# A spectral filter in front of a squared-ReLU FFN: the FFT rebuilt on conjugate pairs, the FFN in 512-token groups over batch borders, one written-out instruction order

## The chip, the cores and the metric

The kernel runs on one core of one Trainium2 chip. The metric is the device time of one execution in microseconds; lower is better. The core has five engines that each work off an instruction list of their own in order: TensorE (PE in the rows; its weight loads are listed apart as PEld), VectorE (DVE), ScalarE (ACT), GpSimd (POOL) and SyncE (SP, which here only issues DMA transfers). They wait for one another through semaphores.

## What is computed

Eight batches of 3008 tokens of 256 channels. Along the tokens of each batch a real FFT is taken, multiplied by a complex filter (one row for each of 1505 frequencies), and transformed back. All 24064 tokens then go through an FFN with a squared ReLU.

```python
def _attn_ref(x, filt_r, filt_i):                 # x: (8, 3008, 256)
    X = np.fft.rfft(x, axis=1)
    F = (filt_r + 1j * filt_i)[None, :, :]        # (1, 1505, 256)
    y = np.fft.irfft(X * F, n=x.shape[1], axis=1)
    return y.astype(np.float32)

def _moe_ref(x, w_in, w_out):                     # (24064, 256), (256, 2048), (2048, 256)
    h = np.maximum(x @ w_in, 0.0)
    return (h * h @ w_out).astype(np.float32)
```

Inputs and output are float32; matmul operands are float16 and sums float32 in both kernels.

## The kernel before

**The FFT as matmuls.** 3008 = 64 x 47. A token is n = 64 n2 + n1, a frequency k = 47 k1 + k2. Every step is a matmul against a constant table:

- *A* (L249, into psA): over n2. x is loaded in four pieces of a batch as x32 (48 rows x 16 x 256 float32, 768 KB, SP, L157), cast to x16 by VectorE (L163, 47x4096), and multiplied by sSA (47x48), 512 columns at a time, 32 matmuls for each batch. ACT copies psA to u (L251), and SP writes u to a DRAM scratch dU (L253, pieces of 384 KB).
- dU is read back with n1 on partitions as ut (L257, two transfers of 768 KB for each batch, in runs of 512 bytes).
- *B* (L275 and L277, into psB): for each of 47 values of k2 two matmuls with 64 output rows and 256 columns, the same table sSB, into the lower and the upper half of psB; 94 for each batch. VectorE multiplies psB by the filter sF into prod (L284, two k2 in one instruction of 128x512). The real Nyquist frequency takes a path of its own (L281, L289, L301).
- *P* (L298, into psP): the inverse over k1, 47 matmuls for each batch; VectorE copies psP to zeta (L302), SP writes it to DRAM as dZ (L304, four transfers of 768 KB).
- dZ is read back as ztw (L308, two transfers of 192 KB for each of eight pieces), and *Y* (L322, into psY) does the inverse over k2: 128 matmuls of 47 columns for each batch. ACT (L326) and VectorE (L329) copy psY to yt, which is the FFN's input with channels on partitions.

**The FFN.** For each batch alone, in groups of 256 tokens (TOKG), 12 to a batch, of which the last has 192. Eight steps g1 with 4 matmuls of 256 columns into psH (L182, two buffers), ACT's relu from psH to h2 (L187), VectorE's square of h2 in place after every second step (L190, 128x1024); then g2, 32 matmuls into psO (L203, one buffer), ACT's copy to ost (L210) and the write to out on ACT's queue (L211).

**The order.** The FFN of batch b-1 is a generator of such steps. While the code of batch b's FFT is written out, `drain(prev, 1)` takes one FFN step after each FFT matmul group, and what is left of the FFN at the end of a batch is written out as one piece; A of batch b needs the x loaded during batch b-1. The tile scheduler may then put instructions of an engine in another order, as its readiness rules have it. Tables and filters are loaded ahead of everything: sSA, sSB, sSBp, sNY, sSAp and then x on SP, the filters (four transfers, since real and imaginary part each stand twice) and the FFN's weights on POOL's queue.

Of the kernel before, what the change touches and what calls it, by code (L numbers as in the profile page):

```python
# [11 lines left out]
AOP = mybir.AluOpType  # L13
# [63 lines left out]
def kernel(
# [27 lines left out]
    p_xin = ctx.enter_context(tc.tile_pool(name="p_xin", bufs=2))  # L105
    p_x16 = ctx.enter_context(tc.tile_pool(name="p_x16", bufs=2))
    p_u = ctx.enter_context(tc.tile_pool(name="p_u", bufs=2))
    p_ut = ctx.enter_context(tc.tile_pool(name="p_ut", bufs=1))
    p_xsb = ctx.enter_context(tc.tile_pool(name="p_xsb", bufs=2))
    p_prod = ctx.enter_context(tc.tile_pool(name="p_prod", bufs=2))  # L110
    p_nyq = ctx.enter_context(tc.tile_pool(name="p_nyq", bufs=1))
    p_zeta = ctx.enter_context(tc.tile_pool(name="p_zeta", bufs=2))
    p_ztw = ctx.enter_context(tc.tile_pool(name="p_ztw", bufs=2))
    p_y = ctx.enter_context(tc.tile_pool(name="p_y", bufs=2))
    p_h2 = ctx.enter_context(tc.tile_pool(name="p_h2", bufs=2))
    p_out = ctx.enter_context(tc.tile_pool(name="p_out", bufs=2))

    sSA = const.tile([47, 48], F16, name="sSA")
    nc.sync.dma_start(out=sSA, in_=dSA.ap())
    sSB = const.tile([128, 47, 66], F16, name="sSB")  # L120
    nc.sync.dma_start(out=sSB, in_=dSB.ap().rearrange("p (a b) -> p a b", b=66))
    sSBp = const.tile([128, 47, 128], F16, name="sSBp")
    nc.sync.dma_start(out=sSBp, in_=dSBp.ap().rearrange("p (a b) -> p a b", b=128))
    sNY = const.tile([1, 128], F16, name="sNY")
    nc.sync.dma_start(out=sNY, in_=dNY.ap())
    sSAp = const.tile([96, 47], F16, name="sSAp")
    nc.sync.dma_start(out=sSAp, in_=dSAp.ap())

    fr3 = filt_r[0:1504, :].rearrange("(k1 k2) d -> k1 k2 d", k2=47)
    fi3 = filt_i[0:1504, :].rearrange("(k1 k2) d -> k1 k2 d", k2=47)  # L130
    sF = const.tile([128, 47, D], F16, name="sF")
    nc.gpsimd.dma_start(out=sF[0:32], in_=fr3)
    nc.gpsimd.dma_start(out=sF[32:64], in_=fi3)
    nc.gpsimd.dma_start(out=sF[64:96], in_=fi3)
    nc.gpsimd.dma_start(out=sF[96:128], in_=fr3)
    sFnyq = const.tile([1, D], F16, name="sFnyq")
    nc.gpsimd.dma_start(out=sFnyq, in_=filt_r[1504:1505, :])

    sWin = const.tile([128, 2, DFF], F16, name="sWin")
    nc.gpsimd.dma_start(out=sWin, in_=moe_w_in.rearrange("(t r) j -> r t j", r=128))  # L140
    sWout = const.tile([128, NJT, 256], F16, name="sWout")
    nc.gpsimd.dma_start(out=sWout, in_=moe_w_out.rearrange("(jt r) c -> r jt c", r=128))

# [222 lines left out]
```

## Time and profile before

| | us |
|---|---|
| runs, median of 3 | 1231.53 |
| runs, lowest to highest | 1229.78 to 1232.30 |
| the profiled execution, first to last instruction (its span) | 1228.8 |
| PE busy in it | 1027.7 |
| ACT busy | 636.9 |
| VectorE busy | 601.2 |

The profile is one execution, and its page gives its span as its time; that is 2.7 us under the median of the runs. "Busy" counts the time in which at least one instruction of the engine is under way. Matmuls are pipelined: the time listed for a group of back-to-back matmuls runs from the first one's start to the last one's modelled end, which lies after the end of its columns. A row's bracket tells how long the engine had been idle before it, and which instruction or transfer ended that.

### The profile page before, as it was taken

The page shows a single profiled execution, that of the slowest core. Times are in us where ns is not written, and L with a number is a line of the kernel's source. Part 1 is how long each engine was busy: PE and PEld are TensorE (multiplying, and loading weights), DVE is VectorE, ACT ScalarE, POOL GpSimd, SP SyncE. Part 2 cuts the span into 40 slices and gives each one's busy share as a digit, 9 for nine tenths or more (in the row PEclk, how much of TensorE's full clock was granted, in tenths as well). Part 3 has the DMA queues.
Part 4 walks back from the last instruction along what each step waited for, and adds up shares of the span by engine and source line. Part 5 has one row for each costly group of instructions (what it writes and reads, how often), then busy time and mean ns, then how long its engine had stood idle before and what let it go on. Part 6 is the DMA issues. An engine that isn't in the chain of part 4 may idle for free.

```text
span 1228.8 us, 20376 instructions
## 1 busy us (share of the span) xinstructions
PE 1027.7 (84%) x8568; PEld 703.8 (57%) x8568; DVE 601.2 (49%) x880; ACT 636.9 (52%) x1193; POOL 4.7 (0%) x11
## 2 busy tenths in 40 slices
PE   0328549999699979997999959997999989997887
PEld 0002115777477757765666637665666757676776
DVE  0216625464257733764359533774358524753332
ACT  0224116665465646455754745555664665455564
POOL 1000000000000000000000000000000000000000
PEclk9999999999799979998999959998899979998999
DMA  9974685135502576127362683146542460242011
GB/s 215 174 159 96 160 147 126 59 93 129 131 27 78 160 151 124 70 94 177 77 117 95 156 172 65 64 131 145 115 77 104 130 144 27 78 129 76 28 34 33
DMA packets 113621, 134.08 MB, mean 109 GB/s; under 512 B 5886, under 2 KB 105726, under 8 KB 110206
## 3 DMA queue, kind: packets, MB, share of 16 engines
q1 hardware_dynamic: 85242, 102.96, 37.1%
q10 hardware_dynamic: 25728, 24.65, 6.3%
q0 software_dynamic: 2560, 5.18, 2.6%
q8 instruction: 67, 1.10, 0.4%
q14 instruction: 24, 0.20, 0.1%
HBM read 75.55 MB, written 62.39 MB: 112 GB/s over the span
## 4 chain that ended last, share of the span: by engine, by line
PE 68%; DMA 12%; ACT 10%; DVE 7%; issue 2%; SPq 1%; ACTq 0%; DVEq 0%
PE psO L203 26%; PE psH L182 23%; ACT h L187 6%; PE psA L249 5%; PE psB L275 5%; DMA x<-in_x_dram 5%; DMA ztw<-dZ 4%; PE psP L298 4%; DVE h L190 3%; PE psY L322 3%; DMA dU<-u 2%; DMA ut<-dU 2%; DVE x L163 1%; ACT u L251 1%; ACT ost L210 1%
## 5 line engine op out<-in xcount | busy, mean ns | idle before, releaser
L187 ACT ACTIVATE h<-psH 128x512 f16<-128x512 f32 (+1 forms) x768 | 433.7, 588 | 154.5 <-PE psH L182 139.6
L182 PE MATMUL psH<-yt,sWin 128*128 128x256 f16 (+1 forms) x3072 | 455.2, 277 | 21.0 <-ACT h L187 15.1
L203 PE MATMUL psO<-sWout,h 128*128 128x256 f16 (+1 forms) x3072 | 418.7, 273 | 8.5 <-DVE h L190 2.4
L190 DVE TENSOR_TENSOR h<-h 128x1024 f16<-128x1024 f16 (+1 forms) x384 | 257.7, 675 | 288.3 <-ACT h L187 287.9
L182 PEld LDWEIGHTS <-sWin 128*128 128x128 f16 x3072 | 290.7, 100 | 111.9 <-issue 72.4
L203 PEld LDWEIGHTS <-h 128*128 128x128 f16 (+1 forms) x3072 | 284.7, 98 | 83.6 <-DVE h L190 35.7
L251 ACT CAST u<-psA 48x512 f16<-48x512 f32 x256 | 141.4, 574 | 124.9 <-PE psA L249 87.6
L284 DVE TENSOR_TENSOR prod<-psB,sF 128x512 f16<-128x512 f32 x192 | 130.1, 678 | 100.2 <-PE psB L277 58.6
L249 PE MATMUL psA<-x,sSA 47*48 47x512 f16 x256 | 110.4, 472 | 65.2 <-DVE x L163 40.4
L210 ACT COPY ost<-psO 128x512 f32<-128x512 f32 x88 | 51.5, 585 | 198.1 <-PE psO L203 198.1
L302 DVE CAST zeta<-psP 128x512 f16<-128x512 f32 x192 | 129.1, 673 | 23.5 <-PE psP L298 22.8
L163 DVE CAST x<-x 47x4096 f16<-47x4096 f32 x32 | 73.0, 2282 | 88.5 <-DMA x<-in_x_dram 48.2
L322 PE MATMUL psY<-sSAp,ztw 96*128 96x47 f16 x1024 | 54.5, 199 | 73.4 <-DMA ztw<-dZ 48.5
L275 PE MATMUL psB<-ut,sSB 128*64 128x256 f16 x376 | 85.5, 306 | 25.1 <-DMA ut<-dU 22.6
L322 PEld LDWEIGHTS <-ztw 96*128 96x128 f16 x1024 | 44.6, 106 | 103.2 <-issue 57.2
L329 DVE CAST yt<-psY 128x376 f16<-128x376 f32 x64 | 35.0, 547 | 119.1 <-PE psY L322 119.1
L249 PEld LDWEIGHTS <-sSA 47*48 47x48 f16 x256 | 22.9, 105 | 114.9 <-issue 105.4
L277 PE MATMUL psB<-ut,sSB 128*64 128x256 f16 x376 | 86.4, 308 | 0.0
L298 PE MATMUL psP<-prod,sSBp 128*128 128x256 f16 x376 | 81.0, 294 | 3.6 <-DVE zeta L302 3.2
L326 ACT CAST yt<-psY 128x376 f16<-128x376 f32 x64 | 30.2, 471 | 94.6 <-PE psY L322 93.3
L275 PEld LDWEIGHTS <-sSB 128*64 128x64 f16 x376 | 29.3, 112 | 71.1 <-issue 70.9
L298 PEld LDWEIGHTS <-sSBp 128*128 128x128 f16 x376 | 33.5, 99 | 25.1 <-issue 16.6
(21 smaller groups left out, 51.3 us busy)
## 6 DMA issues: line engine op xcount, KB each, us to landing
dZ<-zeta SPq DMA_DIRECT2D x32, 768.0 KB, 3.5
ztw<-dZ SPq DMA_DIRECT2D x128, 192.0 KB, 3.4
out_dram<-ost ACTq DMA_DIRECT2D x88, 256.0 KB, 2.2
x<-in_x_dram SPq DMA_DIRECT2D x28, 768.0 KB, 9.2
dU<-u SPq DMA_DIRECT2D x32, 384.0 KB, 4.6
ut<-dU SPq DMA_DIRECT2D x16, 768.0 KB, 9.3
x<-in_x_dram SPq DMA_DIRECT2D x4, 512.0 KB, 8.1
sF<-in_filt_r_dram POOLq DMA_DIRECT2D x2, 752.0 KB, 16.9
```

The source lines that it names most:

```text
L182: nc.tensor.matmul(ps[:, i, 0:tg], sWin[:, dt, jt * 128:(jt + 1) * 128], yt[:, dt, t0:t0 + tg], start=(dt == 0), stop=(dt == 1))
L187: nc.scalar.activation(out=h2[:, jt0:jt0 + 2, 0:tg], in_=ps[:, :, 0:tg], func=AF.Relu)
L190: nc.vector.tensor_mul(out=h2[:, jt0 - 2:jt0 + 2, 0:tg], in0=h2[:, jt0 - 2:jt0 + 2, 0:tg], in1=h2[:, jt0 - 2:jt0 + 2, 0:tg])
L203: nc.tensor.matmul(ps[0:tw, h, :], h2[:, jt, h * 128:h * 128 + tw], sWout[:, jt, :], start=(jt == 0), stop=(jt == NJT - 1))
L249: nc.tensor.matmul(ps, sSA, xt[:, n1a:n1a + 2, :], start=True, stop=True)
L251: nc.scalar.copy(out=u[:, 2 * i:2 * i + 2, :], in_=ps.rearrange("p (a d) -> p a d", d=D))
L275: nc.tensor.matmul(psb[0:64, i, :], sSB[:, k2, 0:64], ut[:, c2, :], start=True, stop=True)
L277: nc.tensor.matmul(psb[64:128, i, :], sSB[:, k2, 0:64], ut[:, c2, :], start=True, stop=True, tile_position=(0, 64))
L284: nc.vector.tensor_mul(out=prod[:, 0:n, :], in0=psb[:, 0:n, :], in1=sF[:, 2 * p:2 * p + n, :])
L298: nc.tensor.matmul(psp[:, i, :], sSBp[:, k2, :], prod[:, i, :], start=True, stop=(k2 != 0))
L302: nc.vector.tensor_copy(out=zeta[:, 2 * pp:2 * pp + n, :], in_=psp[:, 0:n, :])
L322: nc.tensor.matmul(psy[:, j, :], ztc[:, j, dt * 128:(dt + 1) * 128], sSAp, start=True, stop=True)
```

## The change

**FFT.** A token is now n = 32 p + m, m = 0..31 and p = 0..93, that is n1 = 32 h + m with h = p mod 2. x32 has 96 rows x 8 x 256 (768 KB again, 8 KB to a row); x16 is 94x2048; A is 16 matmuls of 94x96 for each batch, and its psA (96x512) is copied by ACT for even units and by VectorE for odd ones. k2 and 47-k2 are taken together as a pair c (24 pairs): their frequencies f fill 64 rows, real and imaginary part 128. B is 24 matmuls of 128x128 by 256 columns. VectorE multiplies psB by the filter in both of its orders (sF now 128 x 2 x 24 x 256, its second order built on the core by four copies of 64x3072), one instruction of 128x1024 for two pairs, psB read twice. P is 48 matmuls of 128x128 by 256 columns, two that add up for each pair; ACT copies psP to ze. dZ shrinks from 128x48x256 to 3072x256 elements. Y is 64 matmuls of 94 columns for each batch. Nyquist sits in row 32 of pair 0, and its path of its own is gone. In bytes loaded at the start: x of batch 0 3.1 MB, tables sSB and sSP 2.4 MB (now on ACT's queue), filters 1.5 MB and FFN weights 2.1 MB in float16 (POOL's queue).

**FFN.** 47 groups of 512 tokens (TG) over all batches; a group over a batch border is split into two column pieces. g1 has 4 matmuls of 512 columns into psH (128x1024, two buffers), one relu of 1024 elements; the square is one instruction for each step; g2 is 8 matmuls of 256 columns into psO (two buffers), for the group before. Output goes out on SP's queue.

**Order.** `manual_schedule` keeps every engine's list as the code writes it. The FFT of batch 0 runs alone. Then 384 slots run, 8 to a group; a slot is ffn_g1, an FFT unit (place 0), ffn_g2 of the group before, an FFT unit (place 1), the output copy if any, the square. The FFT of a batch is laid over 39 slots by `fft_plan`: A in slots 0 to 7, dU's read-back in 8, B in 13 to 24 and P in 14 to 25, dZ's read-back in 27, Y in 31 to 38; it starts at the group in which the batch before begins to be used up.

```diff
-N1 = 64
-N2 = 47
-NK1 = 33
-TOKG = 256
+N1, N2, NC, NM = 64, 47, 24, 32
+TG = 512
+SLOTS = 8
...
+    ctx.enter_context(tc.manual_schedule())
...
+    def psF(name):
+        return pps.tile([128, 512], F32, tag="psF", name=name, bufs=2)
...
+    load_x(0, 0)
+    load_x(0, 1)
+    sSB = const.tile([128, NC, 128], F16, name="sSB")
+    nc.scalar.dma_start(out=sSB, in_=dSB.ap().rearrange("p (a b) -> p a b", b=128))
...
+    def unit_a(b, a):
+        c, i = divmod(a, 4)
+        if i == 0:
+            cast_x(b, c)
+            us[(b, c)] = p_u.tile([96, 8, D], F16, tag="u", name=f"u_{b}_{c}")
+        ps = psF(f"psA_{b}_{a}")
+        nc.tensor.matmul(ps[0:96, :], sSA, x16s[(b, c)][:, 2 * i:2 * i + 2, :],
+                         start=True, stop=True)
...
+        if a % 2 == 0:
+            nc.scalar.copy(out=o, in_=pv)
+        else:
+            nc.vector.tensor_copy(out=o, in_=pv)
+        if i == 3:
+            nc.sync.dma_start(
+                out=dU[b].rearrange("(m q) d -> q m d", q=96)[:, 8 * c:8 * c + 8, :],
+                in_=us.pop((b, c)))
...
+    def read_u(b):
+        ut = p_ut.tile([128, NC, D], F16, tag="ut", name=f"ut_{b}")
+        v = dU[b].rearrange("(p s) d -> p s d", s=NC)
+        for s0, s1 in ((0, 8), (8, 24)):
+            nc.sync.dma_start(out=ut[:, s0:s1, :], in_=v[:, s0:s1, :])
+        uts[b] = ut
...
+        nc.vector.tensor_mul(
+            out=prod,
+            in0=ps.rearrange("p (a d) -> p a d", d=D).unsqueeze(1).to_broadcast([128, 2, 2, D]),
+            in1=sF[:, :, 2 * p:2 * p + 2, :])
...
+        for i in range(2):
+            for v in range(2):
+                nc.tensor.matmul(ps[:, i * D:(i + 1) * D], sSP[:, 2 * p + i, v, :],
+                                 prod[:, v, i, :], start=(v == 0), stop=(v == 1))
...
+        for i in range(2):
+            jt = 2 * s + i
+            for o, b, r, n in segs:
+                for dt in range(2):
+                    nc.tensor.matmul(ps[:, i, o:o + n],
+                                     sWin[:, dt, jt * 128:(jt + 1) * 128],
+                                     yts[b][:, dt, r:r + n],
+                                     start=(dt == 0), stop=(dt == 1))
+        nc.scalar.activation(out=h2[:, 2 * s:2 * s + 2, :], in_=ps, func=AF.Relu)
...
+    def ffn_g2(g, s):
+        t, half = divmod(s, 2)
+        if s % 4 == 0:
+            pso[g] = pps.tile([128, 2, 256], F32, tag="psO", name=f"psO_{g}_{s}", bufs=2)
+        for jt in range(8 * half, 8 * half + 8):
+            nc.tensor.matmul(pso[g][:, t % 2, :], h2s[g][:, jt, t * 128:(t + 1) * 128],
+                             sWout[:, jt, :], start=(jt == 0), stop=(jt == NJT - 1))
...
+        for a in range(16):
+            if a % 4 == 0 and a // 4 + 2 < 4:
+                put(a // 2, 0, load_x, b, a // 4 + 2)
+            put(a // 2, a % 2, unit_a, b, a)
+        put(8, 1, read_u, b)
+        for p in range(12):
+            put(13 + p, 0, unit_b, b, p)
+            put(14 + p, 1, unit_p, b, p)
+        for c in range(4):
+            put(27, 1, read_z, b, c)
...
+        for n in range(16):
+            put(31 + n // 2, n % 2, unit_y, b, n)
...
+    for s in range((NG + 1) * SLOTS):
+        g, k = divmod(s, SLOTS)
+        if g < NG:
+            ffn_g1(g, k)
+        run(work, s, 0)
+        if g > 0:
+            ffn_g2(g - 1, k)
+        run(work, s, 1)
+        if g > 0:
+            ffn_out(g - 1, k)
+        if g < NG:
+            ffn_sq(g, k)
```

**VectorE around a cast of x.** Before, in the FFN of batch 0 (x16_3_0 is the cast of batch 3's first piece, h2 the squares, prod the filter products):

```order
L267 MEMSET zeta_1_3_1780 128x128
L190 TENSOR_TENSOR h2_0_5_1368<-h2_0_5_1368 128x1024
L163 CAST x16_3_0_2391<-x32_3_0_2389 47x4096
L190 TENSOR_TENSOR h2_0_5_1368<-h2_0_5_1368 128x1024
L190 TENSOR_TENSOR h2_0_6_1513<-h2_0_6_1513 128x1024 x3
L284 TENSOR_TENSOR prod_1_15_1650<-psB_1_15_1645,sF_109 128x512
L190 TENSOR_TENSOR h2_0_6_1513<-h2_0_6_1513 128x1024
```

After, in slots 0 to 3 of batch 2's A (u is the copy of an odd psA, h2 the square that closes a slot, x16_2_1 the cast of the second piece):

```order
L203 CAST u_2_0_1371<-psA_2_1_1384 96x512 [waits DMAHW3_49,PE_49]
L297 TENSOR_TENSOR h2_5_1356<-h2_5_1356 128x1024 [waits Activation_49]
L203 CAST u_2_0_1371<-psA_2_3_1409 96x512 [waits PE_49]
L297 TENSOR_TENSOR h2_5_1356<-h2_5_1356 128x1024 [waits Activation_49]
L186 CAST x16_2_1_1426<-x32_2_1_1079 94x2048 [waits DMAHW6_49]
L203 CAST u_2_1_1428<-psA_2_5_1440 96x512 [waits DMAHW4_49,PE_49]
L297 TENSOR_TENSOR h2_5_1356<-h2_5_1356 128x1024 [waits Activation_49]
L203 CAST u_2_1_1428<-psA_2_7_1465 96x512 [waits PE_49]
```

The cast stood far ahead of the A that uses it, among squares and products; it now stands behind the odd copy and the square of the slot before and directly ahead of its A.

**PE around that A.** Before, in a mix of FFN of batch 1 and A of batch 3 (psH and sWin belong to the FFN):

```order
L182 MATMUL psH_1_8_4_3497<-yt_1_735,sWin_116 128x256
L182 LDWEIGHTS sWin_116
L182 MATMUL psH_1_8_4_3497<-yt_1_735,sWin_116 128x256
L249 LDWEIGHTS sSA_99
L249 MATMUL psA_3_1_1_4169<-x16_3_1_2474,sSA_99 48x512
L182 LDWEIGHTS sWin_116
L182 MATMUL psH_1_8_5_3508<-yt_1_735,sWin_116 128x256
L182 LDWEIGHTS sWin_116
```

After, in slot 2 of batch 2's A, at a group over the border of batches 0 and 1 (448 and 64 columns; h2_4 is the group before):

```order
L289 LDWEIGHTS sWin_135
L289 MATMUL psH_5_2_1414<-yt_1_1118,sWin_135 128x64
L196 LDWEIGHTS sSA_111
L196 MATMUL psA_2_4_1429<-x16_2_1_1426,sSA_111 96x512
L304 LDWEIGHTS h2_4_1143
L304 MATMUL psO_4_0_1375<-sWout_137,h2_4_1143 128x256
L304 LDWEIGHTS h2_4_1143
```

An A matmul stood wherever the scheduler found it ready; it now stands between g1 and g2 of a fixed slot.

**SP between A and B.** Before (u_2_3 is the last piece of batch 2's A, ut its read-back):

```order
L308 DMA ztw_1_7_2218<-dZ1_129 48x8x256 [waits DMAHW4_49,DMAHW3_49,PE_49]
L308 DMA ztw_1_7_2218<-dZ1_129 48x8x256 [waits DMAHW0_49]
L253 DMA dU2_122<-u_2_3_2701 48x4096 [waits DMAHW1_49,Activation_49]
L257 DMA ut_2_2822<-dU2_122 64x24x256 [waits DMAHW1_49]
L257 DMA ut_2_2822<-dU2_122 64x24x256
L304 DMA dZ2_130<-zeta_2_0_2868 128x3072 [waits DVE_49]
```

After, at the same place of batch 2:

```order
L205 DMA dU2_97<-u_2_2_1485 96x8x256 [waits DMAHW7_49,DVE_49,Activation_49]
L205 DMA dU2_97<-u_2_3_1540 96x8x256 [waits DMAHW0_49,DVE_49,Activation_49]
L313 DMA out_0_dram<-ost_4_7_1581 128x2x256 [waits DMAHW1_49,Activation_49]
L213 DMA ut_2_1601<-dU2_97 128x2048 [waits DMAHW3_49,DMAHW5_49,DMAHW2_49,DMAHW7_49,DMAHW0_49,PE_49]
L213 DMA ut_2_1601<-dU2_97 128x4096
L313 DMA out_0_dram<-ost_5_3_1649 128x2x256 [waits DMAHW4_49,Activation_49]
```

Output writes have moved onto SP, ahead of and behind the read-back, which waits for the four writes of dU.

## Rows read from the trace of the kernel before

**Rows 1.** The page: busy time of PE and PEld, and the chain by engine.
```profile
PE 1027.7 (84%) x8568; PEld 703.8 (57%) x8568; DVE 601.2 (49%) x880; ACT 636.9 (52%) x1193; POOL 4.7 (0%) x11
...
PE 68%; DMA 12%; ACT 10%; DVE 7%; issue 2%; SPq 1%; ACTq 0%; DVEq 0%
```

**Rows 2.** Timeline, first FFT: start, length, engine, line, instruction [idle before].
```profile
34.42 2.29 DVE L163 CAST x<-x 47x4096 f16<-47x4096 f32 x1 [34.42 <-DMA x<-in_x_dram]
...
94.02 0.39 PE L275 MATMUL psB<-ut,sSB 128*64 128x256 f16 x1 [20.64 <-DMA ut<-dU]
```

**Rows 3.** All psH matmuls: min/median/max ns, first and last start.
```profile
L182 PE MATMUL psH<-yt,sWin x3072: 242/272/422, 196.0 to 1220.8; 128*128 128x256 f16 x176, 128*128 128x192 f16 x16
```

**Rows 4.** Windows: length; PE, PEld, DVE, ACT, POOL busy; granted clock, DMA share, GB/s.
```profile
196.00:330.00 134.00, 121.78 (x1067) 89.70 (x1065) 66.61 (x102) 75.30 (x141) 0.00 (x0) 0.95 0.46 112
1125.00:1229.00 104.00, 89.43 (x752) 70.97 (x750) 31.98 (x47) 58.46 (x106) 0.00 (x0) 0.99 0.09 31
```

**Rows 5.** Timeline of the end, where only the FFN runs.
```profile
1195.37 0.27 PE L203 MATMUL psO<-sWout,h 128*128 128x256 f16 x1
...
1197.49 2.36 PE L203 MATMUL psO<-sWout,h 128*128 128x256 f16 x20
...
1199.89 0.58 ACT L210 COPY ost<-psO 128x512 f32<-128x512 f32 x1 [1.97 <-PE psO L203]
...
1206.04 2.36 PE L203 MATMUL psO<-sWout,h 128*128 128x256 f16 x20
...
1222.18 2.47 PE L203 MATMUL psO<-sWout,h 128*128 128x256 f16 x20 [0.41 <-DVE h L190]
```

**Rows 6.** Timeline, PE alone, where A and Y of two batches meet.
```profile
438.66 0.61 PE L249 MATMUL psA<-x,sSA 47*48 47x512 f16 x2
...
442.02 0.36 PE L322 MATMUL psY<-sSAp,ztw 96*128 96x47 f16 x8 [0.24 <-ACT yt L326]
```

**Rows 7.** Instructions grouped by shape: busy us, mean ns of one, idle before.
```profile
L187 ACT ACTIVATE h<-psH 128x512 f16<-128x512 f32 x704 | 404.0, 597 | 150.4 <-PE psH L182 136.5 <-DVE prod L284 1.0 <-DVE h L190 0.7
...
L182 PEld LDWEIGHTS <-sWin 128*128 128x128 f16 x3072 | 290.7, 100 | 111.9 <-issue 72.4
...
L190 DVE TENSOR_TENSOR h<-h 128x1024 f16<-128x1024 f16 x352 | 240.1, 686 | 259.7 <-ACT h L187 259.5
L251 ACT CAST u<-psA 48x512 f16<-48x512 f32 x256 | 141.4, 574 | 124.9 <-PE psA L249 87.6 <-DMA dU<-u 30.1 <-DMA ztw<-dZ 4.0
L284 DVE TENSOR_TENSOR prod<-psB,sF 128x512 f16<-128x512 f32 x184 | 126.7, 689 | 91.3 <-PE psB L277 58.0 <-PE psP L298 29.0
...
L163 DVE CAST x<-x 47x4096 f16<-47x4096 f32 x32 | 73.0, 2282 | 88.5 <-DMA x<-in_x_dram 48.2 <-PE psA L249 40.3
...
L187 ACT ACTIVATE h<-psH 128x384 f16<-128x384 f32 x64 | 29.7, 491 | 4.1 <-PE psH L182 3.0
```

**Rows 8.** Timeline, VectorE alone: squares back to back.
```profile
296.06 1.74 DVE L190 TENSOR_TENSOR h<-h 128x1024 f16<-128x1024 f16 x3
```

**Rows 9.** DMA issues: count, KB each, median us from issue to landing.
```profile
dZ<-zeta SPq DMA_DIRECT2D x32, 768.0 KB, 3.5
ztw<-dZ SPq DMA_DIRECT2D x128, 192.0 KB, 3.4
...
x<-in_x_dram SPq DMA_DIRECT2D x28, 768.0 KB, 9.2
dU<-u SPq DMA_DIRECT2D x32, 384.0 KB, 4.6
ut<-dU SPq DMA_DIRECT2D x16, 768.0 KB, 9.3
```

**Rows 10.** Windows, columns as in rows 4: the first 20 us.
```profile
0.00:20.00 20.00, 0.00 (x0) 0.11 (x1) 0.00 (x0) 1.28 (x1) 4.71 (x11) 1.00 0.92 223
```

**Rows 11.** Windows, columns as in rows 4: two stretches with gaps on PE.
```profile
300.00:310.00 10.00, 7.51 (x85) 5.61 (x83) 2.22 (x4) 5.01 (x11) 0.00 (x0) 1.00 0.77 140
440.00:450.00 10.00, 4.23 (x66) 2.96 (x65) 3.42 (x5) 2.95 (x6) 0.00 (x0) 0.62 0.54 140
```

More of the change, by code (lines that the diff above doesn't have):

```diff
@@ new lines, in _build_consts @@
+    m = np.arange(NM)
+    SA = np.zeros((N2, 2, 2, 2, NC))
+    for c in range(NC):
+        for h in range(2):
+            SA[:, h, h, 0, c] = np.cos(2 * np.pi * n2 * c / N2)
+            SA[:, h, h, 1, c] = np.sin(2 * np.pi * n2 * c / N2)
+    freq = np.full((NC, 64), -1)
+    for c in range(NC):
+        for j in range(32):
+            freq[c, j] = 47 * j + c
+            if c:
+                freq[c, 32 + j] = 47 * j + 47 - c
+    freq[0, 32] = N // 2
+    SB = np.zeros((NM, 2, 2, NC, 2, 64))
@@ L76 @@
+    SY = np.zeros((2, 2, NC, N2, 2))
+    for c in range(NC):
+        th = 2 * np.pi * c * n2 / N2
+        for i in range(2):
+            SY[i, 0, c, :, i] = np.cos(th)
+            SY[i, 1, c, :, i] = -np.sin(th)
+    f16 = lambda a, p: np.ascontiguousarray(a.reshape(p, -1).astype(np.float16))
+    return f16(SA, 94), f16(SB, 128), f16(SP, 128), f16(SY, 96)
 @with_exitstack
@@ L124 @@
[L124 to L134, printed above, removed]
@@ new lines, with ffn_g1 @@
+    h2s, pso = {}, {}
+    def ffn_g1(g, s):
+        if s == 0:
+            h2s[g] = p_h2.tile([128, NJT, TG], F16, tag="h2", name=f"h2_{g}")
+        h2 = h2s[g]
+        ps = pps.tile([128, 2, 512], F32, tag="psH", name=f"psH_{g}_{s}", bufs=2)
+        segs = []
+        t = g * TG
+        while t < (g + 1) * TG:
+            b, r = divmod(t, S)
+            n = min((g + 1) * TG - t, S - r)
+            segs.append((t - g * TG, b, r, n))
+            t += n
+        for i in range(2):
+            jt = 2 * s + i
[6 more added lines that the diff above has]
+        nc.scalar.activation(out=h2[:, 2 * s:2 * s + 2, :], in_=ps, func=AF.Relu)
@@ new lines, in run @@
+    def run(plan, r, place):
+        for f, a in plan.get((r, place), ()):
+            f(*a)
+    plan0 = fft_plan(0)
+    for r in range(41):
+        if r == 12:
+            for c0, c1 in ((0, 12), (12, 24)):
+                nc.vector.tensor_copy(out=sF[0:64, 1, c0:c1, :], in_=sF[64:128, 0, c0:c1, :])
+                nc.vector.tensor_copy(out=sF[64:128, 1, c0:c1, :], in_=sF[0:64, 0, c0:c1, :])
+        run(plan0, r, 0)
+        run(plan0, r, 1)
+    work = {}
+    for b in range(1, B):
+        first = 0 if b == 1 else ((b - 1) * S // TG) * SLOTS
+        for (r, place), w in fft_plan(b).items():
+            work[(first + r, place)] = w
```

379 lines of the change are left out of this document (133 added, 246 removed).

## The prediction

> **What bounds the kernel now.** I read the page's busy line and chain first. PE is busy 1027.7 of 1228.8 us and the chain of waits gives it 68%, DMA 12% and ACT 10% [rows 1]; what limits it depends on the stage, so I cut the span into stages. Three are to be seen. **First**, nothing of the FFN runs before 196.0 us: x reaches VectorE at 34.4 us, the first B matmul starts at 94.0 us after 20.6 us of waiting for the read-back of dU [rows 2], and the first psH matmul comes at 196.0 us [rows 3]. **Second**, the last 104 us are FFN alone [rows 4], at 8.55 us for 256 tokens: the same run of 20 psO matmuls starts at 1197.49 and 1206.04 us [rows 5]. Those 20 take 2.36 us; the modelled tail of the last is 0.16 us (one alone shows 0.27), so one 256-column matmul costs 0.110 us, and the 64 matmuls of 256 tokens are worth 7.0 us. The missing 1.5 us is PE waiting while ACT clears psH. **Third**, one batch of FFN with the next batch's FFT inside takes some 130 us, PE busy 122 of 134 at a mean granted clock of 0.95 [rows 4]. So PE bounds it in the middle, with too many matmuls there and some holes; round trips through DRAM bound the beginning.
>
> **The change part by part.** From here "slot" is one turn of the new loop: ffn_g1, an FFT unit, ffn_g2, an FFT unit. All sums are for the profiled execution (span 1228.8 us), and 2.7 us are added at the end, the distance from it to the median of the runs (1231.5).
>
> *FFN matmuls.* A slot has 4 matmuls of 512 columns and 8 of 256. Two psA matmuls of 512 columns take 0.61 us [rows 6], less the tail 0.45, so 0.22 each, the same per column as psO. So g1 costs 4 x 0.218 = 0.87 us, g2 8 x 0.109 = 0.87 us, and 376 slots of both (g2 runs one group behind, so that the last 8 slots have only g2 and the first 8 only g1) 376 x 1.747 = **657 us**. Groups of 512 over batch borders remove the 192-token remainders; seven groups are split at a border, into pieces of 64 columns at least. For these and for reaching the high clock I put **6 us** (0 to 12).
>
> *FFT matmuls.* Per batch now 16 psA of 512 columns (32 before), 24 psB of 256 (94 half-wide ones before), 48 psP, 64 psY of 94. With 0.218, 0.109, 0.109, and for psY 0.045 (eight of 47 columns take 0.36 us with the tail [rows 6], 0.025 each; twice the columns cannot be under 0.039), this is 3.5 + 2.6 + 5.2 + 2.9 = 14.2 us, for the seven batches that run inside the FFN **100 us**.
>
> *A rule against this.* Twelve new weight loads stand in each slot, and a load lasts 100 ns in its rows [rows 7]. The 20 psO matmuls each have a load of their own and still come every 0.110 us [rows 5], so loads lie beside matmuls and I cost them at nothing. The Trainium skill ("TensorE: Matmul & The Clock Gate", the section on row/col tiling) says that a load overlaps matmuls in flight only when the row group differs; by that each load here would add its full time. The trace disagrees; what the sum would be by it stands with the rivals.
>
> *What ACT and VectorE must do in a slot.* Relu of 512 elements takes 597 ns and of 384 491 ns [rows 7], 0.83 ns for one more, so 1024 take 1.02 us. ACT has this, one copy (574 ns for 512 elements [rows 7]) and every fourth slot an ost copy: 1.75 us at most. VectorE has the square (686 ns) and in B/P a product of 1024 elements: 689 ns for 512 [rows 7], so at most 1.38 us; together 2.07 us at most. PE's slot is 1.75 us without FFT, 2.18 with A, 2.4 with B and P, 2.15 with Y. In B/P a product starts 0.22 us after its matmuls (ost starts 0.22 us after the last psO has streamed [rows 5]) and ends 1.4 us later, 0.6 us ahead of the matmul that takes its buffer again. There PE stays the bound. ACT is under it everywhere, so that the 1.5 us holes of the tail close: the relu of a slot has the g2 of the same slot beside it.
>
> *The A stretch is another matter.* VectorE's list there is odd copy, square, odd copy, square, cast, and so on, with one cast in two slots. The odd copy needs the slot's last matmul, the square stands behind it, the cast behind that, and the first psA matmul of the next slot needs the cast. PE has only g1 to fill the time, and behind the waiting psA are queued g2 and the whole slot. From the end of the odd matmul: 0.22 to the copy, 0.53 (a PSUM source of 512 elements, the product's 689 ns, less 0.16, since three squares of 686 ns back to back take 1.74 us, 0.53 apart [rows 8]), 0.53 for the square, and a cast of 94x2048, half of the 2282 ns of 47x4096 [rows 7], say 1.2 us: 2.48 us, of which g1 covers 0.87. PE waits 1.6 us. The first cast of a batch has no odd copy ahead of it: the square ends some 1.0 us into the slot, the cast at 2.2, PE wants it at 0.87: 1.3 us. That is 1.3 + 3 x 1.6 = 6.1 us for each of six batches and 4.8 for batch 1: **41 us**. Bounds: 0 if the order on VectorE let the cast through, 55 with no overlap between its instructions.
>
> *DRAM round trips inside the FFN.* After A there are five slots without FFT work, 8.7 us, and g1, 0.9: 9.6 us for the last odd copy (0.9), the dU write (4.6 median) and the first third of ut. ut lands 9.3 us after issue (median of 768 KB pieces), dU 4.6 [rows 9]; the new first piece is 512 KB in rows of 4 KB instead of 512 B, estimate 5 us from there. 10.9 + issue against 9.6: 1.5 us of waiting for each batch, **10 us** (0 to 40). After P the same five slots stand against 0.8 + 3.5 + 3.4 [rows 9]: covered. x pieces (9.2 us) have some 10 us: covered, barely. While SP waits for dU, an out write is queued behind it; three ost buffers of four slots each cover that.
>
> *The first FFT.* x now comes first on SP, the tables on ACT's queue, half as much filter on POOL's. The first 20 us of before move 223 GB/s [rows 10]. 3.1 MB of x alone would be there at 14 us, with all that loads beside it (9.1 MB) at 41; the third and fourth pieces wait for casts, I take 30. A 3, dU and ut 11, B/P 13 turns of 2.0 us (matmuls at half clock 0.43, 0.22, product 1.38) 26, dZ and zt 8, Y 9, and 5 for transfers that share queues: first psH matmul at **92 us** (73 to 115) instead of 196. The filter copies lie in the dU/ut round trip. **End**: last psO to the end of the span now takes 4 us (1222.18 + 2.47 - 0.16 against 1228.8 [rows 5]): **4 us**.
>
> **Sum:** 92 + 657 + 6 + 100 + 41 + 10 + 4 = 910, with the 2.7 us 913 us.
>
> **The rivals.**
> *The casts cost nothing* (the term of 41 falls away, because VectorE is ahead of PE in the A stretch). For it: VectorE's work in two A slots is 3.9 us against PE's 4.4. Against: order, not load, makes the wait. 872 us.
> *Round trips are exposed.* If all of ut must land (9.3 us) before B and zt needs 9 us (its median is 3.4), PE waits 5.5 and 4.5 us for each batch: 70 instead of 10 us, 973 us. For it: PE waited 20.6 us for ut in the first FFT [rows 2].
> *The clock falls in the A stretch*, where I forecast PE busy for about 70% of the time. Granted clock was 1.00 in a stretch with PE busy 7.51 of 10 us, 0.62 (both levels, 1.2 and 2.4 GHz, mixed) with 4.23 [rows 11]; 70% is nearer to the first. At 1.2 GHz eight slots take 17.5 us more, the waits 3.9 less: 82 us for six batches and 8 for batch 1, 1003 us. The Trainium skill (the same page, on oscillation of the clock) describes matmul loops in which a wait in every turn brings the clock down; by it this rival would be the likelier one, but the middle of this trace keeps 1.00 in most stretches with short holes.
> *Slower than before: the weight loads are not hidden.* Place: all 376 slots, with 12 loads of 100 ns, 451 us, and 152 loads for each of seven FFTs, 106 us: 1470 us. It decides from 57% exposed on (319 of 557 us). Against it stand the 0.110 us above.
>
> **How the numbers follow.** Forecast 57%, casts free 15%, round trips 14%, clock 9%, loads 2%, anything else 3%. The range goes from 860 (casts free and the first FFT at 80) to 1000 (round trips and the first FFT at 115), which leaves out the clock, the loads and some of the rest, 15% or so. All but the loads and part of the rest are faster by hundreds of us, far from the 0.2% that a measurement can tell: faster 0.97, within 0.2% 0.01, slower 0.02.
>
> **What would show it.** First psH matmul near 92 us; B/P and plain slots of 2.4 and 1.75 us with PE without holes; in the A stretch PE waiting for the cast, 1.6 us, 21 times, plus the batches' first ones; PE waits for ut under 2 us; granted clock 1.00 from the first FFN slots on. Wrong would be: a first psH after 115 us, PE waits for psH's relu, waits of over 4 us for ut or zt, or a clock under 0.95 in the A stretches.

## The result and the profile after

The changed kernel takes 898.4 us (median, 897.6 to 898.6) against 1231.3 us: 0.729 of the time before, interval 0.727 to 0.731. The forecast was 913 us, within 860 to 1000. The profiled execution spans 896.8 us, 1.6 us under the median of the runs.

The page of the changed kernel, the lines that answer to [rows 1]:

```profile
PE 792.4 (88%) x5952; PEld 552.6 (62%) x5952; DVE 479.1 (53%) x636; ACT 543.6 (61%) x695; POOL 7.9 (1%) x17
...
PE 84%; DVE 6%; DMA 5%; issue 2%; ACT 2%; SPq 0%; DVEq 0%; ACTq 0%
```

PE now makes 84% of the chain, VectorE 6%. All psH matmuls in one row (the answer to [rows 3]), then the stretch in which FFN and FFT run together (windows, columns as in [rows 4]):

```profile
L289 PE MATMUL psH<-yt,sWin x1728: 191/379/634, 91.5 to 884.8; 128*128 128x512 f16 x143, 128*128 128x64 f16 x8, 128*128 128x320 f16 x8, 128*128 128x128 f16 x7
```
```profile
92.00:885.00 793.00, 750.90 (x5729) 527.90 (x5728) 445.29 (x600) 524.21 (x662) 0.00 (x0) 1.00 0.37 112
```

The FFN begins at 91.5 us instead of 196.0, and from there PE is busy 751 of 793 us with the granted clock at 1.00 (2.4 GHz). The column hides that the first 4 us still ran at half of that; the last section comes back to it. Who waited for whom in that part of the span (from 92 us on): engine, for whom, us in total, times, longest:

```profile
ACT h L293 <- PE psH L289: 203.7, 341, 2.4
...
PE psA L196 <- DVE x L186: 41.9, 27, 1.7
...
PE psH L289 <- DVE yt L268: 0.2, 1, 0.2
```

PE's matmuls wait there for one thing, the cast of x: three times in batch 1 and four times in each later batch. The A stretch of batch 2, first on PE, then on VectorE:

```profile
187.70 1.04 PE L289 MATMUL psH<-yt,sWin 128*128 128x448 f16 x8
190.37 0.42 PE L196 MATMUL psA<-x,sSA 94*96 94x512 f16 x1 [1.64 <-DVE x L186]
...
203.62 1.03 PE L289 MATMUL psH<-yt,sWin 128*128 128x512 f16 x4
...
205.36 1.03 PE L289 MATMUL psH<-yt,sWin 128*128 128x512 f16 x4
```
```profile
187.90 0.69 DVE L203 CAST u<-psA 96x512 f16<-96x512 f32 x1 [0.91 <-PE psA L196]
188.50 0.68 DVE L297 TENSOR_TENSOR h<-h 128x1024 f16<-128x1024 f16 x1
189.10 1.22 DVE L186 CAST x<-x 94x2048 f16<-94x2048 f32 x1
191.92 0.69 DVE L203 CAST u<-psA 96x512 f16<-96x512 f32 x1 [1.60 <-PE psA L196]
```

Odd copy, square and cast run one behind the other, with 0.91 and 1.60 us of idle time on VectorE around them: it is not short of time, it is late. The cast ends at 190.32, psA starts at 190.37. Six slots on, without FFT, one slot is 205.36 - 203.62 = 1.74 us and PE has no hole. Instructions by shape and DMA issues, the answers to [rows 7] and [rows 9]:

```profile
L293 ACT ACTIVATE h<-psH 128x1024 f16<-128x1024 f32 x376 | 385.1, 1024 | 206.0 <-PE psH L289 203.7 <-DVE h L297 2.2
...
L186 DVE CAST x<-x 94x2048 f16<-94x2048 f32 x32 | 38.9, 1217 | 23.2 <-DMA x<-in_x_dram 23.2
```
```profile
x<-in_x_dram SPq DMA_DIRECT2D x28, 768.0 KB, 9.1
dU<-u SPq DMA_DIRECT2D x32, 384.0 KB, 3.4
...
ut<-dU SPq DMA_DIRECT2D x8, 1024.0 KB, 6.1
ut<-dU SPq DMA_DIRECT2D x8, 512.0 KB, 3.7
```

### The profile page after: what moved, and what is told of

It is laid out like the page before. It is cut to its first block, busy times and chain, and to the rows that moved or that the text cites. A ratio compares the mean times of both kernels' runs of the same rounds, so it can differ in the third digit from the quotient of the medians.

```text
span 896.8 us, 14010 instructions
## 1 busy us (share of the span) xinstructions
PE 792.4 (88%) x5952; PEld 552.6 (62%) x5952; DVE 479.1 (53%) x636; ACT 543.6 (61%) x695; POOL 7.9 (1%) x17
## 4 chain that ended last, share of the span: by engine, by line
PE 84%; DVE 6%; DMA 5%; issue 2%; ACT 2%; SPq 0%; DVEq 0%; ACTq 0%
PE psO L304 36%; PE psH L289 34%; PE psP L236 5%; DVE x L186 4%; DMA x<-in_x_dram 4%; PE psA L196 3%; PE psB L219 3%; PE psY L259 3%; DVE h L297 2%; ACT ze L238 1%; ACT h L293 1%; DMA dU<-u 1%; DVE u L203 1%; DMA ut<-dU 0%; DMA zt<-dZ 0%
## 5 line engine op out<-in xcount | busy, mean ns | idle before, releaser
L293 ACT ACTIVATE h<-psH 128x1024 f16<-128x1024 f32 x376 | 385.1, 1024 | 206.0 <-PE psH L289 203.7
L304 PE MATMUL psO<-sWout,h 128*128 128x256 f16 x3008 | 388.6, 272 | 0.0
L289 PE MATMUL psH<-yt,sWin 128*128 128x512 f16 (+7 forms) x1728 | 388.1, 352 | 0.2 <-DVE yt L268 0.2
L297 DVE TENSOR_TENSOR h<-h 128x1024 f16<-128x1024 f16 x376 | 258.0, 686 | 188.8 <-ACT h L293 188.8
L304 PEld LDWEIGHTS <-h 128*128 128x128 f16 x3008 | 291.5, 98 | 83.1 <-issue 6.9
L289 PEld LDWEIGHTS <-sWin 128*128 128x128 f16 x1728 | 159.8, 98 | 100.6 <-issue 2.0
L222 DVE TENSOR_TENSOR prod<-psB,sF 128x1024 f16<-128x1024 f32 x96 | 117.4, 1224 | 57.6 <-PE psB L219 56.6
L196 PE MATMUL psA<-x,sSA 94*96 94x512 f16 x128 | 51.4, 421 | 73.9 <-DVE x L186 72.4
L238 ACT CAST ze<-psP 128x512 f16<-128x512 f32 x96 | 56.2, 585 | 68.0 <-PE psP L236 68.0
L201 ACT CAST u<-psA 96x512 f16<-96x512 f32 x64 | 36.9, 577 | 57.8 <-PE psA L196 56.8
L236 PE MATMUL psP<-prod,sSP 128*128 128x256 f16 x384 | 63.0, 290 | 1.6 <-DVE prod L222 0.9
```

What stands on the lines that cost most here:

```text
L196: nc.tensor.matmul(ps[0:96, :], sSA, x16s[(b, c)][:, 2 * i:2 * i + 2, :], start=True, stop=True)
L222: nc.vector.tensor_mul(out=prod, in0=ps.rearrange("p (a d) -> p a d", d=D).unsqueeze(1).to_broadcast([128, 2, 2, D]), in1=sF[:, :, 2 * p:2 ...
L236: nc.tensor.matmul(ps[:, i * D:(i + 1) * D], sSP[:, 2 * p + i, v, :], prod[:, v, i, :], start=(v == 0), stop=(v == 1))
L238: nc.scalar.copy(out=zes[(b, c)][:, 2 * i6:2 * i6 + 2, :], in_=ps.rearrange("p (a d) -> p a d", d=D))
L289: nc.tensor.matmul(ps[:, i, o:o + n], sWin[:, dt, jt * 128:(jt + 1) * 128], yts[b][:, dt, r:r + n], start=(dt == 0), stop=(dt == 1))
L293: nc.scalar.activation(out=h2[:, 2 * s:2 * s + 2, :], in_=ps, func=AF.Relu)
```

## The experiments

Theory: after the change PE's matmuls set the time from 91.5 us on, and the only thing added to them is the wait for the cast, which comes from its place in VectorE's order. Each run has its rival in what was expected of it.

**The cast, one slot earlier** (each cast of a piece c goes to slot 2c-1, ahead of that slot's copy and square).

```diff
         if i == 0:
-            cast_x(b, c)
             us[(b, c)] = p_u.tile([96, 8, D], F16, tag="u", name=f"u_{b}_{c}")
...
+        for c in range(4):
+            put(max(2 * c - 1, first), 0, cast_x, b, c)
...
```

> The cast of each x piece stands one slot earlier on VectorE, ahead of that slot's odd copy and square; nothing else is moved. Theory (PE waits for the cast because of its place in VectorE's order: 41.9 us of psA waits behind casts in the FFN part of the changed kernel): those waits go, and unless another wait takes their place the median falls from 898 to about 857 us. What may be late next are the x pieces 2 and 3 of a batch: their load is issued behind casts 0 and 1, lands 9.1 us later, and the shorter slots leave about 8.7 us; at 2 us for each of seven batches that gives 868 us. Rival (VectorE's amount of work in the A stretch, not its order, holds PE): the waits stay with the copies, 890 us or more.

Measured: 855.1 us (854.6 to 858.2). PE's waits from 95 us on:

```profile
PE psA L195 <- DVE x L186: 1.3, 1, 1.3
PE psA L195 <- DVE u L202: 0.4, 2, 0.2
PE psA L195 <- ACT u L200: 0.3, 1, 0.3
```

41.9 us have become 1.3, and the time fell by 43.3. VectorE does the same work as before, so its amount was not the cause. Nothing was given back. Four casts waited for their x piece, 0.8 us at most, and PE's one wait for a cast is these 1.3 us.

**Casts and x loads far earlier.**

```diff
...
-            cast_x(b, c)
...
+        for c, r in enumerate((-5, -3, 2, 4) if b else (0, 2, 4, 6)):
+            if c < 2:
+                put(max(r, first), 0, load_x, b, c + 2)
+            put(max(r, first), 0, cast_x, b, c)
...
```

> As the run before, but casts 0 and 1 of a batch stand five and three slots ahead of its A stretch, in slots without FFT work or with Y, and casts 2 and 3 two slots ahead of their use, so that the x loads behind them are issued some 10 us earlier too (batch 0 alone keeps its order). Theory: all waits of psA for casts go, 856 us, and if the x pieces were late in the run before, this one is faster than it by as much. Rival (amount of work): 890 us or more.

Measured: 855.4 us (854.9 to 856.0), the same as the run before: one slot is enough.

**No FFT inside the FFN.**

```diff
     for b in range(1, B):
+        yts[b] = yts[0]
+    for b in range(0):
```

> The FFTs of batches 1 to 7 are left out, and the FFN of every batch reads batch 0's y; the first FFT and all 384 slots stay. Theory: slots of 1.74 us without holes, 376 of them, behind 91.5 us, with 4 us of end and some 5 us for the rise of the clock and the groups over borders: 757 us; the FFT inside the FFN is then worth 141 us, 98 for its matmuls and 42 for the casts. Rival (the bare FFN loop has holes of its own that FFT units now fill): 790 us or more.

Measured: 753.9 us (753.3 to 754.5). The slots have no holes of their own: in the part behind the first FFT only psH waits, 0.6 us in all. The FFT inside the FFN is worth 144 us: its matmuls, 42 us of casts, and what the sum below leaves.

**B and P two slots earlier** (three slots of cover for dU and ut instead of five).

```diff
-            put(13 + p, 0, unit_b, b, p)
-            put(14 + p, 1, unit_p, b, p)
+            put(11 + p, 0, unit_b, b, p)
+            put(12 + p, 1, unit_p, b, p)
...
-        if r == 12:
+        if r == 10:
```

> B and P stand two slots earlier, so that three slots instead of five lie between the last A and the first B. By the landings in the trace of the changed kernel (dU 3.4 us, first piece of ut 3.7) the way from the last psA matmul to the first psB is 0.9 + 0.3 + 3.4 + 0.4 + 3.7 = 8.7 us against 6.1 us of cover: 2.6 us of waiting in each of seven batches, 916 us. By the landings that the prediction took (4.6 and 5, 10.9 in all) it is 4.8 us each, 932 us. If the round trip is covered anyway: 898 us.

Measured: 917.6 us (915.2 to 918.9). PE's waits from 95 us on:

```profile
PE psA L196 <- DVE x L186: 41.9, 27, 1.7
PE psB L219 <- DMA ut<-dU: 14.6, 7, 3.2
```

Seven waits, 2.1 us in the mean, near the 2.6 worked out from the landings of the changed kernel and not the 4.8 of the prediction's. So five slots cover the round trip with a margin under one slot, and the prediction's 10 us fell away because dU landed in 3.4 and the first piece of ut in 3.7 us, where it had taken 4.6 and an estimated 5. 19 us were lost for 14.6 of waiting. The rest is about what the clock took: the mean granted clock of the profiled run is 0.994, which is 5 us (an estimate, 0.006 of 917 us), and the three stretches in which it falls lie behind waits for ut. Behind the first of these, of 3.25 us, the eight psO matmuls of a slot take 1.91 us instead of 1.04.

**g1 in 256 columns** (eight loads and matmuls where four were).

```diff
-            n = min((g + 1) * TG - t, S - r)
+            n = min((g + 1) * TG - t, S - r, 256 - (t - g * TG) % 256)
```

> Each matmul of g1 is cut into two of 256 columns with the same weights, each with a weight load of its own: 8 loads and matmuls in a slot's g1 instead of 4. Theory (loads lie beside matmuls; a matmul costs its columns and 2 to 3 ns): four more matmuls for each of 376 slots at 2.5 ns, 4 us, 902 us. Rival (each load adds its 98 ns): 376 x 4 x 0.098 = 147 us more, 1045 us.

Measured: 901.9 us, 3.5 us more. The 1472 more matmuls and weight loads (3200 against 1728 of this line) cost 2.4 ns each: the loads lie beside the matmuls. Four plain slots of the trace take 6.99 us here and 6.95 in the changed kernel.

**The tile scheduler's order.**

```diff
-    ctx.enter_context(tc.manual_schedule())
```

> The line that keeps the written order is taken out, so that the tile scheduler orders every engine's list, as it did in the kernel before; FFT, groups of 512 and tables stay. Theory (the shorter FFT at the beginning and PE's work are one part of the gain, 105 and some 60 us, the holes that the fixed slots close the larger rest): time is given back in the FFN part, 950 to 1060 us. Rival (the order is worth nothing, since the code is written in that order anyway): 880 to 905 us; faster than 898 if the scheduler lets the casts go ahead of the copies.

Measured: 864.5 us (864.2 to 865.0), faster than the written order by 34 us, and slower by 9 than that order with the cast one slot earlier. My theory, that time is given back without the fixed order, has fallen; but this run does not undo the interleaving. In an A stretch PE still goes through g1, psA, g2 and psA as the code writes them; what is new is VectorE's list, which here goes square, odd copy, cast and not odd copy, square, cast. First PE, then VectorE, then PE's waits from 95 us on:

```profile
182.46 1.04 PE L288 MATMUL psH<-yt,sWin 128*128 128x448 f16 x8
183.33 0.40 PE L195 MATMUL psA<-x,sSA 94*96 94x512 f16 x1
183.56 1.04 PE L303 MATMUL psO<-sWout,h 128*128 128x256 f16 x8
```
```profile
184.58 0.69 DVE L296 TENSOR_TENSOR h<-h 128x1024 f16<-128x1024 f16 x1 [0.78 <-ACT h L292]
185.19 0.68 DVE L202 CAST u<-psA 96x512 f16<-96x512 f32 x1
185.79 1.21 DVE L185 CAST x<-x 94x2048 f16<-94x2048 f32 x1
```
```profile
PE psB L218 <- DMA ut<-dU: 6.1, 5, 2.3
```

No wait for a cast is left. The 41.9 us that these waits cost are gone, 6.1 us of waiting for ut and 3.4 of a later first psH matmul have come, which is about the 34: the price of the casts' place once more. What the run loses to the run with the early cast is these 6.1 us and a first psH matmul at 94.9 us. What the slots as such are worth, no run shows.

**The FFN's weights after x** (a one-element copy from the last x piece on GpSimd holds the loads back).

```diff
-    nc.gpsimd.dma_start(out=sWin, in_=moe_w_in.rearrange("(t r) j -> r t j", r=128))
...
+        if r == 6:
+            nc.gpsimd.tensor_copy(out=sWin[0:1, 0, 0:2], in_=x16s[(0, 3)][0:1, 0, 0:2])
+            nc.gpsimd.dma_start(out=sWin, in_=moe_w_in.rearrange("(t r) j -> r t j", r=128))
+            nc.gpsimd.dma_start(out=sWout, in_=moe_w_out.rearrange("(jt r) c -> r jt c", r=128))
```

> The loads of the FFN's weights on POOL's queue wait for the last x piece of batch 0, so that they no longer run beside it (2.1 MB, issued at 20.7 us, while the fourth piece of x takes 15.7 us to land). Theory (the fourth piece is late because it shares the queues): it lands some 6 to 8 us earlier, the first psH matmul comes at 84 instead of 91.5 us, 891 us. Rival (the pieces are late for their own chain of casts, or the time is given back when dU and ut share with the weights instead): 898 us.

Measured: 899.1 us (897.8 to 900.3), no gain: the rival. The cast of the last x piece, first in the changed kernel, then in this run; below them what PE waited for ut in all, in the same order:

```profile
36.93 1.22 DVE L186 CAST x<-x 94x2048 f16<-94x2048 f32 x1 [6.51 <-DMA x<-in_x_dram]
```
```profile
33.23 1.22 DVE L184 CAST x<-x 94x2048 f16<-94x2048 f32 x1 [2.65 <-DMA x<-in_x_dram]
```
```profile
PE psB L219 <- DMA ut<-dU: 10.6, 1, 10.6
```
```profile
PE psB L217 <- DMA ut<-dU: 15.0, 1, 15.0
```

x landed 3.7 us earlier, and the wait for ut grew by 4.4: the weights only moved beside the next transfers on the way.

**Groups of 256 in the new order.**

```diff
-TG = 512
+TG = 256
...
-        for jt in range(8 * half, 8 * half + 8):
+        for jt in range(4 * quarter, 4 * quarter + 4):
...
-            work[(first + r, place)] = w
+            work[(first + 2 * r + place, 0)] = w
```

> Groups of 256 tokens in the new order: slots of half the work, one FFT unit in each, relu of 512 elements, square of 512, psH of one bank; the FFT stays as laid out in time. Theory (PE is the bound in every slot, and ACT's 2 x 0.6 us for the same 1024 elements stays under it): 900 to 915 us. Rival (larger instructions carry the gain; groups of 256 leave ACT's hole of 1.5 us for 256 tokens that the kernel before had at its end): 94 x 1.5 = 141 us more, 1039 us.

Measured: 901.8 us (901.5 to 902.4), 3.5 us more. The size of the groups is worth no more than that, and the sum has other parts: g1 has as many matmuls here as in the run with 256 columns, which lost the same 3.5 us; the granted clock is 0.83 from 90 to 110 us where the changed kernel has 1.00 (some 3 us, an estimate from 0.17 of 20 us); and the waits for casts are 38.1 us instead of 41.9.

**g2 in a lump.**

```diff
-    for s in range((NG + 1) * SLOTS):
+    for s in range(NG * SLOTS):
         g, k = divmod(s, SLOTS)
...
+        if k == SLOTS - 1:
+            for kk in range(SLOTS):
+                ffn_g2(g, kk)
+                ffn_out(g, kk)
```

> The changed kernel with g2 in one lump: the 64 matmuls of a group's g2 stand behind the eight slots of its own g1 instead of in eight pieces beside the next group's g1, as in the kernel before. Theory (the gain in the FFN is that ACT's relu has g2 beside it): in eight slots without g2 PE has 0.87 us and ACT about 1.0, with FFT units 1.5 and 1.6, so g1 waits for psH, and at the end of a group g2 waits some 0.9 us for the last squares: 1.6 to 1.9 us for each of 47 groups, 975 to 985 us. Rival (the lump costs nothing, since FFT units fill the holes): 898 to 910 us.

Measured: 964.8 us (964.5 to 964.9), 66 us more, 1.4 us for each group; I had said 1.6 to 1.9. The lump on PE, and ACT beside it:

```profile
261.73 7.15 PE L304 MATMUL psO<-sWout,h 128*128 128x256 f16 x64
...
265.42 0.59 ACT L311 COPY ost<-psO 128x512 f32<-128x512 f32 x1 [3.19 <-PE psO L304]
```

For 7 us ACT has hardly more than two output copies; then g1 without g2 meets an ACT that takes longer than PE. In the slots without FFT just ahead of this lump PE waits for the relu:

```profile
256.40 1.94 PE L289 MATMUL psH<-yt,sWin 128*128 128x512 f16 x8 [0.25 <-ACT h L293]
258.53 1.94 PE L289 MATMUL psH<-yt,sWin 128*128 128x512 f16 x8 [0.20 <-ACT h L293]
```

Eight psH matmuls come every 2.13 us, where their columns need 1.73 and two relus 2.05. This is the part of the gain in the FFN that the runs show best; how the 66 us divide over slots with and without FFT is not shown.

**g2 in pieces, in the kernel before** (an FFN step is a g1 and four matmuls of the g2 of the group before).

```diff
...
+                def unit(g1=g1, jp=jp, g=g):
+                    if g < ngt:
+                        g1()
+                    if g > 0:
+                        st[g - 1](jp)
+                yield unit
...
```

> The kernel before with one part of the change: an FFN step now holds a g1 and four matmuls of the g2 of the group before, instead of g2 as a lump of 32; FFT, groups of 256, batches and scheduler stay. Theory (the lump makes ACT's hole of 1.5 us for 256 tokens at the end of the kernel, and part of it in the middle): 12 groups at the end give 18 us, the other 84 groups half of it or less, since FFT work fills holes there: 1150 to 1213 us. Rival (the middle is held by something else, and the end by PE): 1225 us or more.

Measured: 1221.9 us against 1231.5, ratio 0.992 (0.990 to 0.995): 10 us, less than the 18 at least that the theory gave. The same six psH matmuls of two groups at the end of this run, 256 tokens apart; then windows from the first psH matmul to the start of the last psY group and from there to the end, first in the kernel before and then here:

```profile
1160.56 0.82 PE L184 MATMUL psH<-yt,sWin 128*128 128x256 f16 x6
...
1167.78 0.82 PE L184 MATMUL psH<-yt,sWin 128*128 128x256 f16 x6
```
```profile
196.00:1120.40 924.40, 848.33 (x7404) 603.40 (x7402) 498.56 (x751) 528.51 (x995) 0.00 (x0) 0.95 0.43 109
1120.40:1228.80 108.40, 93.74 (x776) 73.75 (x775) 33.22 (x49) 60.31 (x109) 0.00 (x0) 0.97 0.09 29
```
```profile
198.00:1125.50 927.50, 848.67 (x7405) 620.06 (x7402) 504.26 (x751) 546.77 (x995) 0.00 (x0) 0.91 0.44 108
1125.50:1218.90 93.40, 87.67 (x776) 75.42 (x775) 33.23 (x49) 61.40 (x109) 0.00 (x0) 0.98 0.10 34
```

At the end the theory holds: 256 tokens take 7.22 us where they took 8.55, and the end is 15 us shorter. But the first psH matmul comes 2 us later and the middle takes 3 us longer: the gain that was hoped for there did not come. PE's wait for ztw over the run, first in the kernel before, then here:

```profile
PE psY L322 <- DMA ztw<-dZ: 48.5, 19, 15.3
```
```profile
PE psY L333 <- DMA ztw<-dZ: 61.6, 23, 16.2
```

An FFN that PE can work off faster leaves longer holes where Y waits for DRAM (21.4 and 22.0 us of these sums lie in the first FFT, so inside the FFN 27.1 us have become 39.6), and the mean granted clock of the profiled run falls from 0.956 to 0.928. In the middle, what one part gives, another takes.

**The FFN held back, in the kernel before.**

```diff
-                drain(prev, 1)
+                drain(prev, i % 2)
```

> The kernel before with every second FFN step taken out of the A stretch, so that 16 more steps of a batch's FFN are left for the stretch in which Y of the next batch waits for the read-back of dZ. Theory (the FFN of a batch runs out before Y of the next is done: PE idles there 10 us or so in each of six batches, and the granted clock falls to 0.5 to 0.7 for 20 us): 60 to 130 us less, 1100 to 1170 us. Rival (the scheduler moves FFN ahead as before, or the holes appear in A instead): 1215 us or more.

Measured: 1186.9 us, ratio 0.964 (0.962 to 0.965): 45 us, less than the 60 to 130. The mechanism is there. In the kernel before, the last psO of batch 1 is done at 438.7 us and the last psY group of batch 2 starts at 452.2; here both start within 0.3 us of each other, at 435.5 and 435.2 us. Where the kernel before had PE busy 4.23 of 10 us at a clock of 0.62 [rows 11], this run has

```profile
420.00:450.00 30.00, 28.32 (x268) 19.89 (x268) 14.31 (x19) 21.40 (x46) 0.00 (x0) 1.00 0.49 119
```

and the wait for ztw fell to

```profile
PE psY L322 <- DMA ztw<-dZ: 26.2, 7, 16.2
```

with a mean granted clock of 0.985. 23.0 us of what is left belong to the first FFT, which has no FFN beside it; inside the FFN 27.1 us have become 3.2.

**Early cast and late weights together** (the weights wait for the second part of ut).

```diff
...
+        if r == 13:
+            nc.gpsimd.tensor_copy(out=sWin[0:1, 0, 0:2], in_=uts[0][0:1, 8, 0:2])
+            nc.gpsimd.dma_start(out=sWin, in_=moe_w_in.rearrange("(t r) j -> r t j", r=128))
...
```

> The cast one slot early as in the first run (855 us), and the loads of the FFN's weights wait until all of ut of batch 0 has landed, so that they run beside B and P, when the DMA queues are nearly empty, and not beside x, dU or ut. Theory (in the run that only let them wait for x, the fourth x piece was 3.7 us earlier and the gain went to dU and ut, which then shared with the weights): first psH matmul at 83 to 86 instead of 91.1 us, 848 to 850 us. Rival (the round trip of dU and ut costs the same without the weights): 855 us.

Measured: 849.1 us (848.1 to 851.5), 0.690 of the kernel before (0.688 to 0.691) and 5.5% under the changed kernel, the fastest of all. Its psH row:

```profile
L286 PE MATMUL psH<-yt,sWin x1728: 191/379/634, 83.7 to 837.7; 128*128 128x512 f16 x143, 128*128 128x64 f16 x8, 128*128 128x320 f16 x8, 128*128 128x128 f16 x7
```

7.4 us earlier than in the run with the early cast alone (91.1). 6.0 us of them reach the time: in batch 1's A stretch one x piece comes late here, PE waits 2.9 us for its cast, and the granted clock of the window from 84 to 104 us is 0.85. The loads of the weights cost least behind x, dU and ut, where nothing urgent was under way.

## Why the prediction was right, step by step

| term | forecast, us | measured, us | from |
|---|---|---|---|
| first FFT | 92 | 91.5 | first psH matmul |
| FFN slots | 657 | 654 | 376 x 1.74 |
| FFT matmuls | 100 | 98 | below |
| casts | 41 | 41.9 | waits |
| dU and ut | 10 | 0 | waits |
| borders, rise of the clock | 6 | 7 | what is left |
| end | 4 | 4 | 896.8 less 884.98 + 8.02 - 0.16 |
| to the median | 2.7 | 1.6 | runs against span |

FFT matmuls: two B/P slots and the end of the FFN on PE:

```profile
214.04 0.38 PE L219 MATMUL psB<-ut,sSB 128*128 128x256 f16 x2
216.43 0.38 PE L219 MATMUL psB<-ut,sSB 128*128 128x256 f16 x2
...
884.98 8.02 PE L304 MATMUL psO<-sWout,h 128*128 128x256 f16 x72
```

A B/P slot is 2.39 us, 0.65 over the plain one; 12 of them are 7.8, 16 psA at 0.22 are 3.5, and Y slots of 2.08 us (248.81 to 250.89 us in the trace) add 0.34 each, 2.7 for eight: 14.0, seven times.

- **PE's matmul rate** held: loads are hidden, as the 20 psO matmuls of [rows 5] had shown and the run with g1 in 256 columns confirmed. The rule of the Trainium skill that was weighed there ("TensorE: Matmul & The Clock Gate", the section on row/col tiling) is not borne out by either.
- **ACT under PE** held: relu takes 1024 ns where 1.02 us were worked out, and psH never waits for it. That the 1.5 us of the old end lay between PE and ACT, the run with g2 in pieces in the kernel before shows: 8.55 us became 7.22, against 7.0 of matmuls.
- **The wait for the cast** held in mechanism and size: 1.64 us where 1.6 were forecast, and 1.23 for the first cast of a batch where it was 1.3. Reading where an instruction stands in an in-order list, and what the engine behind it still has in hand, was enough. The two runs with early casts show the cause.
- **The clock** stayed at 1.00 in the A stretch with PE waiting 1.64 us in every 6.2, so that rival did not come. It was not far: behind a wait of 3.25 us, with B and P two slots earlier, matmuls ran at half speed. The loops that the Trainium skill describes (the same page, the section "HAM oscillation") wait longer in each turn than PE does here, so the page spoke less for this rival than the prediction made of it.
- **DRAM round trips** were mis-sized: 10 us forecast, none measured, because dU (3.4 us) and ut's first piece (3.7) landed sooner than the rows of before (4.6, and an estimate of 5) had it. It is the largest part of the 15 us by which the forecast was too high; 3 came from the slots and 1 from the distance between span and median.
- **The first FFT** was right in its sum, and its parts partly cancelled: the last x piece arrived at 36.9 us and not at 30, psB started at 51.3, Y began at 83.1. A turn of B and P took 2.1 us where 2.0 were forecast, but that is luck: the forecast put VectorE's product (1.38 us) at its end, and the trace shows VectorE idle for 0.89 us in each turn and psB waiting for ACT's copy of psP, which the forecast did not have:

```profile
58.66 0.59 PE L219 MATMUL psB<-ut,sSB 128*128 128x256 f16 x2 [0.67 <-ACT ze L238]
```
```profile
59.28 1.23 DVE L222 TENSOR_TENSOR prod<-psB,sF 128x1024 f16<-128x1024 f32 x1 [0.89 <-PE psB L219]
```

**Where the 333 us came from.** 104.5 us are the first FFT (196.0 to 91.5). Of the other 228, the g2 in pieces accounts for 66 in the new kernel; holding the FFN back, so that it still runs when Y waits for DRAM, is worth 45 in the old one. The size of the groups is worth 3.5 us at most, and the fixed order, with the cast where it stands, costs 34 against the scheduler's. The rest, over 100 us, includes the interleaving of the slots, which no run undoes as a whole, fewer FFT matmuls and the end at which the old FFN had no work beside it; it is not split by a run. Nor need parts add up: g2 in pieces is worth 66 us in the new kernel and gave the old one 10. That the worth of a part depends on the others is shown for this part only.

## What to carry to other kernels

When the order is written by hand, look for an instruction that stands behind a consumer of the same slot's last result and ahead of a producer for the next slot's first: here a 1.2 us cast cost 1.6 us of the busiest engine each time, and one slot earlier it cost nothing. A lump of one kind of work leaves the other engines idle even where there is other work to interleave, but taking the lump apart paid little in the old kernel, where the round trips behind it were not covered. Before giving the credit to one part of a change, undo that part alone, and read in the trace what the run undid: without the line that fixes the order PE kept the written slots in the stretch that was read, and what went away was the price of the misplaced casts.

## What the hardware showed that I had not expected

The granted clock reads 1.00 from the start of the span, yet the matmuls of the first FFT run at half of full speed: in the changed kernel the first four psB matmuls of 256 columns take 1.01 us, 0.21 each, against 0.38 us for two later, 0.11 each.

```profile
51.27 1.01 PE L219 MATMUL psB<-ut,sSB 128*128 128x256 f16 x4 [10.56 <-DMA ut<-dU]
```

0.21 us for 256 columns is 1.2 GHz. The rise does not show either: four psH matmuls of 512 columns take 1.42 us at 94.40 and 1.03 us at 96.09, and the column reads 1.00 for both. So at the start of a span the spacing of matmuls says more than the column. Also, a copy of 64x3072 from float16 to float16 took 955 ns, 0.31 ns for each element of a row, where the cast of x from float32 took 0.59.
